# Buffers of the exponentials as slices of one lasting tile, with the order between two exponentials of a slice declared

## The chip, the cores and the metric

The kernel runs on one core of a Trainium2 chip. A core has five engines that run at the same time and wait for each other by semaphores: TensorE (PE, matmuls, with the loading of its weights shown apart as PEld), VectorE (DVE), ScalarE (ACT), GpSimd (POOL) and SyncE (SP, which here issues the DMAs). The metric is device time of one execution in microseconds (us); shorter is better. All times below are of one core.

## The reference

The input x has 2048 rows of 512. The kernel computes `x + s * g`, where s is an attention over the normalized rows and g comes from an MLP over the same rows.

```
xn = layernorm(x)
q  = (xn @ wq) as 32 heads of 16;  k = xn @ wk;  v = xn @ wv      # one k and v for all heads
p  = softmax(q k^T / 4)                                            # 32 heads x 2048 x 2048
s  = (p v, heads side by side) @ wo
h  = xn @ w1 + b1                                                  # 2048 x 1792
g  = silu((h * tanh(softplus(h))) @ w2)
out = x + s * g
```

All numbers are float32.

## The kernel before, in words

**Tiling.** Rows are taken in 4 blocks (C = 512 rows). The 32 heads go in 8 groups of four, so there are 4 x 8 = 32 units (block, group), and each unit goes over the 2048 keys in 16 tiles of 128. One unit and one key tile are one *step*: 512 steps. In each step four score tiles of 128 keys by 512 rows are made, one for each head of the group, exponentiated, and two steps later multiplied with the values.

**What a step issues.** The program is written out by hand in the order in which each engine runs it (manual schedule). For most of the kernel a step holds on TensorE:

- four score matmuls `e` (line 881), each on 64 of the array's rows, into PSUM tiles of the pool `ps_e`, which has three banks;
- four matmuls `m` (line 904) on the other half of the rows, for the running maxima of a later unit, into the pool `ps_m` (three banks); VectorE reduces each of them (line 908);
- a share of one other matrix product, `xps` (line 113), in halves of 64 rows: the projection to q, the two products of the MLP, and the product with `wo`. Such a product is a *group* of 12 or 15 matmuls into the one bank of `ps_x`, cut into chunks of at most 8, and each chunk takes two steps, one for each half of the rows;
- the four value products `pv` of two steps before (line 958), on all rows, which read four exponentials.

The function `waves` interleaves the first three kinds, so that the `e`, `m` and `xps` matmuls of the two row halves run side by side; the value products stand behind them.

ACT takes the exponential of each score tile (line 886, out of PSUM into an SBUF buffer `pt`, 128 x 512). Behind the four exponentials of a step it has one or two other jobs: the stages of the MLP's activation (lines 658, 667, 671), the sigmoid of the gate (727, 732, 737), the reciprocal of the softmax sums (982, 986). Where a group of products ends, ACT or DVE empties its bank between exponentials (lines 597, 652, 715, 719), and once per unit ACT empties the bank of the value products (line 967).

**The buffers of the exponentials.** Before the change, each exponential takes a new tile from a pool with 14 buffers (`NPT = 14`, tag `pt`). The framework that places semaphores makes a new tile wait for everything that used its buffer before: the value products that read it, and the older exponential that wrote it.

```
pt = sb.tile([P, C], F32, tag="pt", name=f"pt{s}_{i}", bufs=NPT)
r = act.activation(pt, e, AF.Exp, scale=0.25)
pt_of[16 * v + k, p, a] = pt
```

In the last 20 steps or so, two of the exponentials of every fourth step go to other buffers (`qh`, `ql`). At the start of the kernel the same 14 buffers hold the first 14 row tiles of x (`load_x`), before any exponential is made.

**The start and the end.** Before the steps begin, a lead of some 90 us (planned with the costs of `Task` objects) normalizes x and computes k, v and the first q. Its weights and the kernel's later ones are loaded, split into a high and a low part, and kept in DRAM. The last 22 steps have no `m` matmuls; the last product with `wo` ends the kernel.

Of the kernel before, what the change touches and what calls it, by code (L numbers as in the profile page):

```python
# [14 lines left out]
F32 = mybir.dt.float32  # L15
# [5 lines left out]
P = 128  # L21
S = 2048
D = 512
# [4 lines left out]
C = 512  # L28
# [15 lines left out]
NPT = 14  # L44
# [75 lines left out]
def block_kernel(ctx: ExitStack, tc: tile.TileContext, x, wq, wk, wv, wo, w1, b1, w2, out):  # L120
    nc = tc.nc
    cp = ctx.enter_context(tc.tile_pool(name="const", bufs=1))
    sb = ctx.enter_context(tc.tile_pool(name="work", bufs=2))
# [65 lines left out]
    nbias = cp.tile([P, NKT], F32, name="nbias")  # L189
    b1c = cp.tile([P, NFT], F32, name="b1c")  # L190
    wbs = cp.tile([P, 5, 2, D], F32R, name="wbs")
    ot_all = cp.tile([P, 4, 2, C], F32R, name="ot_all")

    xr = x.rearrange("o (t p) d -> (o t) p d", p=P)
# [11 lines left out]
    xin = {}  # L206

    def load_x(c):
        for tt in range(4):
            tag, n = ("pt", NPT) if 4 * c + tt < NPT else (("y0", "sc")[tt % 2], 1)  # L210
            xin[c, tt] = sb.tile([P, D], F32, tag=tag, name=f"xin{c}_{tt}", bufs=n)
            sp.dma_start(xin[c, tt], xr[4 * c + tt])

    mvs = cp.tile([P, NKT, 2], F32, name="mvs")
# [26 lines left out]
    def x_scale(t):  # L241
        x_ = xin[divmod(t, 4)]
        if t < 4:
            dve.tensor_scalar(x_, x_, rstd[:, t:t + 1], nbias[:, t:t + 1], op0=ALU.mult, op1=ALU.add)  # L244
        else:
            xn_scale(x_, x_, t)
# [72 lines left out]
    def v_out(c):  # L319
        dve.tensor_copy(vaug[:, 4 * c:4 * c + 4, 0:DH], vp_of[c][:, :, 16:32])  # L320

    load_x(0)
    wkv = sb.tile([P, C], F32, tag="xr", name="wkv", bufs=4)
    wkv = wkv[:, 0:2 * NDT * DH].rearrange("p (a t n) -> p a t n", a=2, t=NDT)
# [56 lines left out]
    def arrived(tag):  # L381
        k, n = todo[tag]
        return k < n and items[tag][k].step + 1 <= (step[0] if lead else max(step[0], busy[0] / STEP_US) + 0.3)
# [459 lines left out]
    def take(n):  # L843
        r = [m1s.popleft() for _ in range(min(n, len(m1s)))]
        queue.extend(r)
        return r

    take(AHEAD)
    for c in range(NC):
        for k in range(3):  # L850
            a = take(2)
# [11 lines left out]
    queue.extend(wo_groups(NC - 1))  # L863

    pt_of = {}
    pv_of = {}
    mb_of = {}
    o_of = {}

    def e_one(s, i):  # L870

        v, r = divmod(s, 16)
        if s < NS - LEAD:
            a, k, p = 1 - s % 2, r - r % 2 + i // 2, i % 2
        else:
            a, k, p = i % 2, r, i // 2
        q = qt_of[v]
        o = 64 * a
        ps, tag = (ps_m, "m") if NS - LEAD <= s and i in ((1, 3) if s < NS - 8 else (3,)) else (ps_e, "e")
        e = ps.tile([P, C], F32, tag=tag, name=f"e{s}_{i}")  # L880
        pe.matmul(e, ks[o:o + 64, P * k:P * (k + 1)], q[o:o + 64, p], start=True, stop=True)  # L881
        if i > 1 and s % 4 == 1 and PAIRS[0] < s < PAIRS[1]:
            pt = sb.tile([P, C], F32, tag=("qh", "ql")[i - 2], name=f"pt{s}_{i}", bufs=1)
        else:
            pt = sb.tile([P, C], F32, tag="pt", name=f"pt{s}_{i}", bufs=NPT)
        r = act.activation(pt, e, AF.Exp, scale=0.25)  # L886
        pt_of[16 * v + k, p, a] = pt
        return r

    m_next = [0, 0]  # L890
# [29 lines left out]
    def c_rows(v):  # L920

        mp = sb.tile([P, 2, 3, 8], F32R, tag="mp", name=f"mp{v}", bufs=2)
        mx = f(mp[:, :, 0])
        w = {}

        def reduce():
            dve.reduce_max(out=mx, in_=mb_of[v].rearrange("p b (a z) -> p a z b", a=2), axis=AX.X)

        def parts():
            dve.tensor_reduce(out=mp[:, :, 1], in_=mx.rearrange("p a (z o) -> p a z o", o=1), axis=AX.X,  # L930
                              op=ALU.max, negate=True)
            dve.tensor_reduce(out=f(mp[:, :, 2]), in_=f(mp[:, :, 0:2]).rearrange("p a s z -> p a z s"), axis=AX.X,
                              op=ALU.add, negate=True)

        def turn():
            cr = w["cr"] = sb.tile([P, 32], F32, tag="cr", name=f"cr{v}", bufs=2)
            dve.transpose(cr, f(mp[:, :, 1:3]).rearrange("p a s z -> p a (s z)"))

        def move():
            q, cr = qt_of[v], w["cr"]  # L940
            for a in range(1, -1, -1):
                r = 64 * a + 48
                for b in range(4):
                    sp_at(0.68)
                    sp.dma_start(f(q[r:r + 2]).rearrange("o p (t b n) -> b o (p t) n", b=4, n=32)[b],
                                 cr[32 * b + 16 * a:32 * b + 16 * a + 16])
        return reduce, parts, turn, move

    def pv(s):
        v, k = divmod(s, 16)  # L950
        if k == 0:
            pv_of[v] = ps_v.tile([P, C], F32, tag="v", name=f"pv{v}")
        o = pv_of[v]
        for p in range(2):
            for a in range(2):
                pt = pt_of.pop((s, p, a))
                j = 2 * p + a
                pe.matmul(o[32 * j:32 * j + 32], vaug[:, k], pt, start=(k == 0), stop=(k == 15))  # L958

# [108 lines left out]
    def task(eng, us, fn, deps=(), **kw):  # L1068
        t = Task(eng, us, fn, deps, **kw)
        plan[eng].append(t)  # L1070
        return t
# [30 lines left out]
    xat = {t: landed(DMA_US) for t in range(4)}  # L1102
    load("wq")
    load_x(1)
    xat.update({t: landed(DMA_US) for t in range(4, 8)})
    load("ws")
    sp.dma_start(b1c, b1.rearrange("(t p) -> p t", p=P))
    load_x(2)
    load_x(3)
    xat.update({t: landed(DMA_US) for t in range(8, 16)})  # L1110
# [18 lines left out]
    for c0, c1 in ((0, 1), (1, 2), (2, 4)):  # L1129
        z = slice(4 * c0, 4 * c1)  # L1130
# [3 lines left out]
        for c in range(c0, c1):  # L1134
            xs, his = [], []
            for t in range(4 * c, 4 * c + 4):
                sc = task(*(("ACT", 0.72), ("DVE", 0.4))[c == 0], lambda t=t: x_scale(t), [nrm])
# [75 lines left out]
    while True:  # L1213
# [21 lines left out]
        s, e, k = min(opts, key=lambda o: o[0])  # L1235
# [5 lines left out]
        if k == "M":  # L1241
# [7 lines left out]
            if vdone[0] == 0 and min(m_next) >= m_need(0):  # L1249
                vdone[0] = 1  # L1250
                r = c_rows(0)
# [20 lines left out]
        elif k == "J":  # L1272
            tag = next((g for g in ("wq", "ws", "wb") if arrived(g) and busy[0] + E0 < s + 0.5), None)
            n = ran[0]
# [16 lines left out]
    while left:  # L1291
        k = next(k for k in left if all(d.end is not None for d in k.deps))
# [6 lines left out]
    for s in range(NS + 2000):  # L1299
        inm = s < NS - LEAD  # L1300
        if inm or cur["chunk"]:
# [4 lines left out]
            def em(k):  # L1306
                n = m_sides(1 - h, k // 2) if inm else 0
                x = deque(lambda i=i: e_one(s, i) for i in range(4))
                y = deque(lambda: m_one(1 - h) for _ in range(n))
                r = [[], []]  # L1310
                for op in EM:
                    if op == "M" and y:
                        r[1 - h].append(y.popleft())
                    elif op == "E":
                        r[1 - h].append(x.popleft())
                r[h] = [lambda: m_one(h) for _ in range(4 - n if inm else 0)]
                return r
# [6 lines left out]
            if s >= 2:  # L1324
                pv(s - 2)
                if (s - 1) % 16 == 0 and s > 1:
                    o_out((s - 17) // 16)
        elif PAIRS[0] <= s < PAIRS[1]:
            due(s)
            if s % 2 == 0:  # L1330
                es = [(s + n // 4, n % 4) for n in range(8)]
                for n in es[:6]:
                    e_one(*n)
                fill(8)
                act_jobs(4)
                for n in es[6:]:
                    e_one(*n)
                for n in range(s - 2, s):
                    pv(n)
                if s % 16 == 0:  # L1340
                    o_out(s // 16 - 1)
            due(s + 0.5)
        else:
# [6 lines left out]
            if s <= NS:  # L1350
                pv(s - 2)
                if s == NS:
                    pv(s - 1)
                if s == NS or (s - 1) % 16 == 0:
                    o_out((s - 16) // 16)
# [4 lines left out]
        if vdone[0] < 8 * NC and min(m_next) >= m_need(vdone[0]):  # L1360
            r = c_rows(vdone[0])
# [20 lines left out]
```

## Time and profile before

| | |
|---|---|
| median of 3 runs | 1609.91 us (1608.72 to 1612.72) |
| the profiled execution | 1610.56 us |
| its span, first to last instruction | 1608.7 us |
| mean granted TensorE clock | 0.998 |
| VectorE, the row maxima of `m` (line 908) | 2048 instructions, 682 ns each in the mean |
| ACT, exponentials (line 886) | 2048 instructions, 606 ns each in the mean |
| TensorE, the products `xps` (line 113) on the chain that ended last | 48% |
| TensorE, the value products (line 958) on it | 31% |

How to read it: the profile has a page of one execution. "Busy" is the time in which an engine runs at least one instruction; instructions of an engine's own sequencer (waits on semaphores, branches, issuing of DMAs) are not busy time and are marked with a q (ACTq, PEldq). Matmul ends are modelled, and matmuls overlap, so that a busy TensorE can still be waiting. The chain that ended last is followed back from the last instruction, at each step to what released it. The order of time lists instructions with start and duration in us; a bracket tells how long the engine was idle before and what ended that. In a view of one line, three numbers with slashes are the shortest, median and longest duration in ns.

### The profile page before, as it was taken

What the parts mean: (1) busy time and instruction counts of PE and PEld (TensorE: products, weight loads), DVE (VectorE), ACT (ScalarE), POOL (GpSimd) and SP (SyncE); (2) the same over time, 40 slices, a digit from 0 to 9 for tenths busy, and PEclk for the clock granted to TensorE, in tenths of its full rate; (3) what the DMA queues carried; (4) which work ended last, traced back from release to release, by engine and by line L of the source; (5) the groups of instructions that cost most, each with busy time, mean ns of one, the idle gap of its engine ahead of it and who ended that gap; (6) DMA issues with size and microseconds to landing.
All of it is one profiled execution on the core that took longest, in us unless ns stands there. A gap on an engine that the chain in (4) does not pass through costs nothing.

```text
span 1608.7 us, 31578 instructions
## 1 busy us (share of the span) xinstructions
PE 1590.6 (99%) x11660; PEld 853.1 (53%) x11660; DVE 1345.7 (84%) x2299; ACT 1292.6 (80%) x2490; POOL 620.0 (39%) x628
## 2 busy tenths in 40 slices
PE   8999999999999999999999999999999999999998
PEld 5455555555555555555555555555555555555543
DVE  8988888888988888888898988888889898888811
ACT  5468788789898778978889787887898878789785
POOL 3786158155365102422524222251251414225312
PEclk9999999999999999999999999999999999999999
DMA  5332133142131315112113231230332213031020
GB/s 161 145 116 83 33 108 119 30 149 76 35 134 61 94 37 173 59 32 87 51 55 96 67 99 37 97 102 16 122 97 83 70 47 106 16 108 45 8 86 27
DMA packets 72778, 127.33 MB, mean 79 GB/s; under 512 B 21488, under 2 KB 34288, under 8 KB 72112
## 3 DMA queue, kind: packets, MB, share of 16 engines
q1 hardware_dynamic: 72624, 125.30, 24.5%
q8 instruction: 93, 1.52, 0.4%
q14 instruction: 61, 0.50, 0.1%
HBM read 76.36 MB, written 27.26 MB: 64 GB/s over the span
## 4 chain that ended last, share of the span: by engine, by line
PE 95%; DVE 2%; ACT 1%; POOL 1%; issue 0%; DMA 0%; SPq 0%; DVEq 0%; ACTq 0%; POOLq 0%
PE xps L113 48%; PE pv L958 31%; PE m L904 8%; PE e L881 5%; PE xps L109 2%; PE kp L293 1%; PE wop L109 1%; DVE mb L908 1%; PE warm L1191 0%; ACT pt L886 0%; ACT xin L198 0%; DMA xin<-in_dram 0%; DVE st L218 0%; POOL hb L157 0%; DVE xin L244 0%
## 5 line engine op out<-in xcount | busy, mean ns | idle before, releaser
L908 DVE TENSOR_REDUCE mb<-m 128x1 f32<-128x512 f32 x2048 | 1272.1, 682 | 189.6 <-PE m L904 162.9
L886 ACT ACTIVATE pt<-e 128x512 f32<-128x512 f32 x2048 | 1068.7, 606 | 255.2 <-PE e L881 243.2
L904 PE MATMUL m<-ks,qt 48*128 48x512 f32 (+1 forms) x2048 | 840.6, 421 | 0.6 <-DVE mb L908 0.2
L881 PE MATMUL e<-qt,ks 64*128 64x512 f32 x2048 | 749.1, 408 | 1.4 <-ACT pt L886 1.4
L958 PE MATMUL pv<-pt,vaug 128*32 128x512 f32 x4096 | 543.8, 604 | 0.0
L904 PEld LDWEIGHTS m<-ks,qt 48*128 48x128 f32 (+1 forms) x2048 | 371.7, 185 | 52.6 <-DVE mb L908 19.0
L881 PEld LDWEIGHTS e<-qt,ks 64*128 64x128 f32 x2048 | 372.9, 186 | 24.3 <-ACT pt L886 17.3
L113 PE MATMUL xps<-xt,ws 64*128 64x512 f32 x1248 | 346.0, 410 | 1.9 <-POOL ws L157 0.9
L113 PE MATMUL xps<-wbs,act 64*128 64x512 f32 x1248 | 337.3, 407 | 0.0
L113 PEld LDWEIGHTS xps<-xt,ws 64*128 64x128 f32 x1248 | 215.1, 185 | 207.5 <-ACT pt L886 135.8
L113 PEld LDWEIGHTS xps<-wbs,act 64*128 64x128 f32 x1248 | 217.6, 185 | 179.9 <-ACT pt L886 112.4
L958 PEld LDWEIGHTS pv<-pt,vaug 128*32 128x32 f32 x4096 | 81.4, 108 | 143.3 <-issue 134.4
L167 POOL TENSOR_SCALAR t<-t 128x512 f32<-128x512 f32 x56 | 34.4, 615 | 316.2 <-ACT t L658 316.1
L157 POOL TENSOR_TENSOR hb<-hb,t 128x512 f32<-128x512 f32 x56 | 72.2, 1289 | 77.8 <-ACT t L671 55.2
L113 PE MATMUL xps<-xt,wq 64*128 64x512 f32 x336 | 93.0, 409 | 0.0
L113 PEld LDWEIGHTS xps<-xt,wq 64*128 64x128 f32 x336 | 57.9, 185 | 55.7 <-ACT pt L886 35.2
L157 POOL TENSOR_TENSOR oc<-oc,sc 128x512 f32<-128x512 f32 (+1 forms) x16 | 20.6, 1288 | 162.4 <-ACT sc L986 96.7
L113 PE MATMUL xps<-wbs,ot_all 64*128 64x512 f32 x288 | 79.3, 407 | 0.0
L113 PEld LDWEIGHTS xps<-wbs,ot_all 64*128 64x128 f32 x288 | 49.4, 184 | 47.1 <-ACT pt L886 29.3
L157 POOL TENSOR_TENSOR hb<-hb,u 128x512 f32<-128x512 f32 x56 | 72.2, 1290 | 4.4
L157 POOL TENSOR_TENSOR act<-hb,act 128x512 fp32r<-128x512 f32 x56 | 72.0, 1286 | 4.7
L157 POOL TENSOR_TENSOR u<-u,t 128x512 f32<-128x512 f32 x56 | 71.8, 1282 | 4.7
(113 smaller groups left out, 807.4 us busy)
## 6 DMA issues: line engine op xcount, KB each, us to landing
ws<-w SPq DMA_DIRECT2D x38, 512.0 KB
wbs<-w SPq DMA_DIRECT2D x36, 512.0 KB
qt<-qh SPq DMA_DIRECT2D x256, 32.0 KB
w<-ws SPq DMA_DIRECT2D x14, 512.0 KB
w<-wbs SPq DMA_DIRECT2D x14, 512.0 KB
wq<-wq SPq DMA_DIRECT2D x13, 512.0 KB
wbs<-wo SPq DMA_DIRECT2D x12, 512.0 KB
rawwb<-in_dram SPq DMA_DIRECT2D x20, 256.0 KB
```

Of the source, the lines that this page charges most:

```text
L109: self.pe.matmul(ps, self.lhs(), self.rhs(), start=(self.k == 0), stop=(self.k == self.tot - 1))
L113: i = self.pe.matmul(ps, self.lhs()[o], self.rhs()[o], start=(self.k == 0 and self.halves == 0), stop=(self.k == self.tot - 1 and self.hal ...
L157: eng.tensor_tensor(out=o, in0=a, in1=b, op=op)
L167: pool.tensor_scalar(o, o, lim, 0.0, op0=ALU.min, op1=ALU.max)
L293: pe.matmul(kp_of[c], wkf[:, dt], xf_of[c][dt // 2][:, dt % 2], start=(dt == 0), stop=(dt == 3))
L881: pe.matmul(e, ks[o:o + 64, P * k:P * (k + 1)], q[o:o + 64, p], start=True, stop=True)
L886: r = act.activation(pt, e, AF.Exp, scale=0.25)
L904: pe.matmul(m, q[o, p, P * t:P * (t + 1)], ks[o, C * kb:C * (kb + 1)], start=True, stop=True)
L908: return dve.reduce_max(out=mb_of[v][:, kb, z:z + 1], in_=m, axis=AX.X)
L958: pe.matmul(o[32 * j:32 * j + 32], vaug[:, k], pt, start=(k == 0), stop=(k == 15))
```

## The change

The 14 pool buffers of the exponentials become slices of one tile `pts` that lasts through the kernel. The program hands the slices out itself: an exponential takes the one that has been free the longest (`pt_free`), and the value product that reads a slice gives it back. For each slice the last exponential is remembered (`pt_last`), and the next exponential in that slice is declared to have no dependency on it, since the value products that read the slice lie between the two. The wait on those value products stays. The first 14 row tiles of x are loaded into the same slices.

```
+    pts = cp.tile([P, NPT, C], F32, name="pts")
...
-            tag, n = ("pt", NPT) if 4 * c + tt < NPT else (("y0", "sc")[tt % 2], 1)
-            xin[c, tt] = sb.tile([P, D], F32, tag=tag, name=f"xin{c}_{tt}", bufs=n)
+            if 4 * c + tt < NPT:
+                xin[c, tt] = pts[:, 4 * c + tt]
+            else:
+                xin[c, tt] = sb.tile([P, D], F32, tag=("y0", "sc")[tt % 2], name=f"xin{c}_{tt}", bufs=1)
...
+    pt_last = {}
+    pt_free = deque(range(NPT))
...
+        z = None
         if i > 1 and s % 4 == 1 and PAIRS[0] < s < PAIRS[1]:
             pt = sb.tile([P, C], F32, tag=("qh", "ql")[i - 2], name=f"pt{s}_{i}", bufs=1)
         else:
-            pt = sb.tile([P, C], F32, tag="pt", name=f"pt{s}_{i}", bufs=NPT)
+            z = pt_free.popleft()
+            pt = pts[:, z]
         r = act.activation(pt, e, AF.Exp, scale=0.25)
-        pt_of[16 * v + k, p, a] = pt
+        if z in pt_last:
+            tc.declare_no_dep(r.ins, pt_last[z].ins, reason="the value products that read the tile lie between")
+        if z is not None:
+            pt_last[z] = r
+        pt_of[16 * v + k, p, a] = pt, z
...
-                pt = pt_of.pop((s, p, a))
+                pt, z = pt_of.pop((s, p, a))
+                if z is not None:
+                    pt_free.append(z)
```

## The prediction

> **What bounds the kernel now.** I read the page first: share of each engine, then the chain that ended last.
>
> ```profile
> PE 1590.6 (99%) x11660; PEld 853.1 (53%) x11660; DVE 1345.7 (84%) x2299; ACT 1292.6 (80%) x2490; POOL 620.0 (39%) x628
> ...
> PE 95%; DVE 2%; ACT 1%; POOL 1%; issue 0%; DMA 0%; SPq 0%; DVEq 0%; ACTq 0%; POOLq 0%
> PE xps L113 48%; PE pv L958 31%; PE m L904 8%; PE e L881 5%; PE xps L109 2%; PE kp L293 1%; PE wop L109 1%; DVE mb L908 1%; PE warm L1191 0%; ACT pt L886 0%; ACT xin L198 0%; DMA xin<-in_dram 0%; DVE st L218 0%; POOL hb L157 0%; DVE xin L244 0%
> ...
> L886 ACT ACTIVATE pt<-e 128x512 f32<-128x512 f32 x2048 | 1068.7, 606 | 255.2 <-PE e L881 243.2
> ```
>
> Read alone, this says that TensorE is full and that the exponentials (ACT, line 886) have 255 us of idle time ahead of them, so that nothing done to them can matter. But a busy PE is not PE at its peak, and matmul ends are modelled, so I went down to the order of time. Next the view of line 886:
>
> ```profile
> L886 ACT ACTIVATE pt<-e x2048: 577/602/695, 92.5 to 1593.5; 128x512 f32<-128x512 f32 x187
> L886 ACTq EVENT_SEMAPHORE  x344: 17/17/38, 108.9 to 1542.9; - x172
> ```
>
> 344 of the 2048 exponentials have an instruction of ACT's sequencer of their own ahead of them. An exponential must wait for its score matmul in any case; I read the 344 as those that have a second wait beside it, nearly all of them on the older exponential in the buffer. Now two steps in a row, in the order of time; the columns are start and duration in us. First one whose exponentials have no such instruction:
>
> ```profile
> 625.01 0.18 PEld L113 LDWEIGHTS xps<-xt,ws 64*128 64x128 f32 x1 [0.84 <-ACT pt L886]
> 625.36 0.40 PE L881 MATMUL e<-qt,ks 64*128 64x512 f32 x1
> 625.80 0.60 ACT L886 ACTIVATE pt<-e 128x512 f32<-128x512 f32 x1 [0.79 <-PE e L881]
> ...
> 626.45 0.18 PEld L881 LDWEIGHTS e<-qt,ks 64*128 64x128 f32 x1
> 626.53 0.41 PE L881 MATMUL e<-qt,ks 64*128 64x512 f32 x1
> 626.87 0.16 PEld L958 LDWEIGHTS pv<-pt,vaug 128*32 128x32 f32 x8 [0.24 <-issue]
> ...
> 627.86 0.18 PEld L113 LDWEIGHTS xps<-xt,ws 64*128 64x128 f32 x1 [0.84 <-ACT pt L886]
> ```
>
> and the next one, which has it ahead of its first exponential (at 628.6):
>
> ```profile
> L886 ACTq EVENT_SEMAPHORE  x1: 17/17/17, 628.6 to 628.6; - x1
> ...
> 628.21 0.40 PE L881 MATMUL e<-qt,ks 64*128 64x512 f32 x1
> 628.70 0.60 ACT L886 ACTIVATE pt<-e 128x512 f32<-128x512 f32 x1 [0.24 <-PE e L881]
> ...
> 629.35 0.18 PEld L881 LDWEIGHTS e<-qt,ks 64*128 64x128 f32 x1
> 629.38 0.46 PE L881 MATMUL e<-qt,ks 64*128 64x512 f32 x1
> 629.77 0.16 PEld L958 LDWEIGHTS pv<-pt,vaug 128*32 128x32 f32 x8 [0.24 <-issue]
> ...
> 630.77 0.18 PEld L113 LDWEIGHTS xps<-xt,ws 64*128 64x128 f32 x1 [0.84 <-ACT hb L652]
> ```
>
> Follow the loop. The first score matmul of the step ends at 625.36 + 0.40 = 625.76; the first exponential starts 0.04 later and ends at 626.40. The step's fourth score matmul needs the PSUM bank that this exponential empties (three banks carry four score tiles): its weight load starts at 626.45, 0.05 after that end. The value products start 0.42 after that load, and the next step's first weight load 0.99 after them. From the first weight load to the next one it is 2.85. In the second step the exponential starts 0.09 after its matmul's end (628.61 to 628.70), everything behind it keeps its distance (fourth load 0.05 after the exponential's end at 629.30, value products 0.42 on, next step 1.00 on), and the step takes 2.91. So in these steps the PE, busy as it looks, stands in a loop with ACT: the delay from the first score matmul's end to the first exponential's start is on the path, one for one.
>
> Not all steps are so. Where the group of products that runs beside has 15 of them (parts of the second MLP product) the PE has more to do per step:
>
> ```profile
> 586.05 0.18 PEld L113 LDWEIGHTS xps<-wbs,act 64*128 64x128 f32 x1 [0.84 <-ACT pt L886]
> ...
> 589.13 0.18 PEld L113 LDWEIGHTS xps<-wbs,act 64*128 64x128 f32 x1 [0.84 <-ACT pt L886]
> ...
> 592.18 0.18 PEld L113 LDWEIGHTS xps<-wbs,act 64*128 64x128 f32 x1 [0.84 <-ACT pt L886]
> ...
> 595.22 0.18 PEld L113 LDWEIGHTS xps<-wbs,act 64*128 64x128 f32 x1 [0.84 <-ACT y L715]
> ...
> L886 ACTq EVENT_SEMAPHORE  x3: 17/17/17, 593.0 to 596.0; - x3
> ```
>
> These are 3.04 to 3.08 apart, the last one with the extra instruction ahead of its first exponential (at 593.0), the others without: there the delay is hidden.
>
> **The change part by part.** *The wait that goes.* Sorting the 485 steps from 99.9 to 1524 us by whether the value products start 0.47 after the first exponential's end (the loop above) gives 359 looped steps and 126 with the PE as their limit. Of the looped ones 167 have the extra instruction ahead of an idle first exponential, the first and the last of them being
>
> ```profile
> 108.45 0.39 PE L881 MATMUL e<-qt,ks 64*128 64x512 f32 x1
> ...
> 108.94 0.60 ACT L886 ACTIVATE pt<-e 128x512 f32<-128x512 f32 x1 [0.27 <-PE e L881]
> ...
> 1478.74 0.40 PE L881 MATMUL e<-qt,ks 64*128 64x512 f32 x1
> ...
> 1479.24 0.60 ACT L886 ACTIVATE pt<-e 128x512 f32<-128x512 f32 x1 [0.23 <-PE e L881]
> ```
>
> and 172 have none, from the first to the last:
>
> ```profile
> 99.92 0.39 PE L881 MATMUL e<-qt,ks 64*128 64x512 f32 x1
> 100.35 0.60 ACT L886 ACTIVATE pt<-e 128x512 f32<-128x512 f32 x1 [0.17 <-PE e L881]
> ...
> 1484.50 0.40 PE L881 MATMUL e<-qt,ks 64*128 64x512 f32 x1
> ...
> 1484.94 0.60 ACT L886 ACTIVATE pt<-e 128x512 f32<-128x512 f32 x1 [0.28 <-PE e L881]
> ```
>
> Over the 167 the delay from matmul end to exponential start is 0.102 us in the mean, over the 172 it is 0.046: 0.056 apart. Their lengths say the same: median 2.907 against 2.852, 0.055 apart. The term is 167 x 0.056 = 9.4 us. Twelve more looped steps have the extra instruction behind an ACT job that ends late; they are worth between nothing and 12 x 0.056 = 0.7, and I take 0.3, as the job hides most of it. The 79 PE-limited steps with the instruction give nothing (above), and so do the instructions ahead of a third exponential, which has ACT work before it.
>
> What is late next? In a step without the instruction the fourth load still starts 0.05 behind the exponential's end, so ACT stays the limit there at 2.85; the 172 such steps show that the PE can run at that length.
>
> One rule of the Trainium skill prices this differently. The row gives the instruction 17 ns; the page "Perfetto Trace Analysis", in the timeline of a sequencer-only instruction, says that the reported window is the execution alone and leaves the wait and the tail out. If the 17 ns were all, the term would be 167 x 0.017 = 2.8 us; the 0.056 measured between the two kinds of step agrees with the page.
>
> *The tile.* The 14 buffers become 14 slices of one lasting tile of the same bytes; the loads of x land in the same slices. No instruction is added: 0. The first exponential in each slice keeps its wait on what the lead did there, 14 of 2048: 0. The free list hands slices out in the order in which the value products gave them back, one step and more before; those products stand in PE's queue ahead of the score matmul that the exponential waits for, so this wait is carried by that one: 0. Dependencies that are kept by tile and not by slice would cost a great deal; that is a rival.
>
> *Waits that others may inherit.* An exponential that waited for an older one told ACT's later instructions that this was done; some may now need a wait of their own. Nearest rows: ACT's other jobs that run between exponentials,
>
> ```profile
> L652 ACT ACTIVATE hb<-xps,b1c 128x512 f32<-128x512 f32 x56 | 38.7, 690 | 9.8 <-PE xps L109 9.8
> ...
> L967 ACT ACTIVATE os<-pv 128x512 f32<-128x512 f32 x31 | 18.7, 603 | 5.1 <-PE pv L958 2.6
> ```
>
> Between 0 and 87 x 0.056 = 4.9 us. I take 0: their buffers come round only after many steps, and jobs of the same chain wait on ACT in between; other jobs run behind the fourth exponential, where ACT then idles 0.23 to 0.28 (rows above) and 0.056 is covered.
>
> Sum: 9.4 + 0.3 = 9.7 off the profiled execution's own 1610.56 us (span 1608.7 and 1.9 around it) gives 1600.9. That execution lies 0.65 above the median 1609.91 of the three; I let the number stand against its own execution.
>
> **The rivals.** (1) *The wait is not what I take it for, or something else takes its place.* If the 344 instructions have another second wait, nothing changes: 1610.6. If 87 evacuations inherit it: 1610.6 - 9.7 + 4.9 = 1605.8, within 0.3%. For: no row names the semaphore of those instructions. Against: 2048 - 344 = 1704 exponentials run without, so score matmul and buffer need no second wait by themselves. 0.10 for both. (2) *ACT is not the bound, so nothing moves*, as the shares at the top say. The Trainium skill, page "Perfetto Trace Analysis", section "Identifying the Most-Contended Engine", has the engine of highest occupancy optimized first, which is not ACT here (PE 99%, DVE 84%, ACT 80%). Against it stand the two steps above, 2.85 and 2.91 with the same PE work. 1610.6, chance 0.02. (3) *Slower: the one lasting tile is tracked whole.* Then the value products, issued behind the step's four exponentials, wait for the last of them instead of starting 0.47 after the first one's end.
>
> ```profile
> 637.30 2.06 ACT L886 ACTIVATE pt<-e 128x512 f32<-128x512 f32 x4 [0.28 <-PE e L881]
> ...
> L437 SPq DMA_DIRECT2D wbs<-w x36: 326/418/1344, 548.1 to 1428.5; - x36
> ```
>
> Four exponentials take 2.06, the first 0.60, so the last ends 1.46 behind the first: products 1.0 later in each of 485 steps, 1610.6 + 485 = some 2096. It decides as soon as a read of one slice waits for a write of another. Against: the ring of wbs is a lasting tile with five slices, refilled by 36 DMAs while products read other slices, and no wait of the PE on those DMAs is listed. 0.04. (4) *All first exponentials gain*, also the PE-limited 79 and the 12: 258 x 0.056 = 14.4, 1596.1. Against: the 3.04 to 3.08 above. 0.05.
>
> **How the numbers follow.** My forecast has 0.79. About 0.3% (4.8 us) is what a measurement of this kernel can tell from no change. Faster: 0.79 + 0.05 = 0.84. Same: 0.10 + 0.02 = 0.12. Slower: 0.04. The range reaches from the fourth rival's 1596.1 to the inherited waits' 1605.8: 1596 to 1606.
>
> **What would show it.** Right: the row of sequencer instructions at line 886's exponential falls from 344 to a handful; the first exponential starts about 0.04 after its matmul in nearly all looped steps, which then take 2.85, and 15-product steps stay at 3.04 to 3.08; ACT's idle time behind score matmuls falls by some 10 us; DVE, POOL and DMA counts stay. Wrong: the row stays; or it falls and steps stay at 2.91, which would put the limit elsewhere; or new sequencer instructions stand at lines 652 and 967; or the value products start behind the fourth exponential.

## The result and the profile after

The changed kernel takes 1599.99 us in the median of six runs (1597.75 to 1602.72), against 1609.84 for six runs of the kernel before: a ratio of 0.9938, 95% interval 0.9925 to 0.9951. The profiled execution takes 1599.22 us, 1597.4 of it in its span.

First the page, with the rows that answer to those shown of before. The engines' shares hardly tell the two kernels apart:

```profile
PE 1579.5 (99%) x11660; PEld 843.1 (53%) x11660; DVE 1345.5 (84%) x2299; ACT 1292.7 (81%) x2490; POOL 620.1 (39%) x628
...
PE 93%; DVE 2%; POOL 2%; ACT 2%; DMA 1%; issue 0%; SPq 0%; DVEq 0%; POOLq 0%; ACTq 0%
...
L893 ACT ACTIVATE pts<-e 128x512 f32<-128x512 f32 x2042 | 1065.5, 605 | 245.7 <-PE e L886 237.2
```

TensorE is "busy" for 11.1 us less, with the same 11660 matmuls: busy time that was waiting. ACT's idle time ahead of the exponentials fell from 255.2 to 245.7. The view of the exponential's line, now 893:

```profile
L893 ACT ACTIVATE pts<-e x2042: 577/600/697, 90.2 to 1582.2; 128x512 f32<-128x512 f32 x186
L893 ACT ACTIVATE pt<-e x6: 579/594/599, 1530.1 to 1553.7; 128x512 f32<-128x512 f32 x6
L893 ACTq EVENT_SEMAPHORE  x3: 17/38/38, 1527.6 to 1530.1; - x3
```

Of the 344 sequencer instructions three are left, all at the end; in the kept trace these three wait for DMAs and stand there in the kernel before as well. And the two steps that the prediction showed, in the order of time (start and duration in us):

```profile
619.40 0.18 PEld L113 LDWEIGHTS xps<-xt,ws 64*128 64x128 f32 x1 [0.84 <-ACT pts L893]
...
619.74 0.40 PE L886 MATMUL e<-qt,ks 64*128 64x512 f32 x1
...
620.18 0.60 ACT L893 ACTIVATE pts<-e 128x512 f32<-128x512 f32 x1 [0.78 <-PE e L886]
...
621.63 0.61 ACT L893 ACTIVATE pts<-e 128x512 f32<-128x512 f32 x1
...
622.25 0.18 PEld L113 LDWEIGHTS xps<-xt,ws 64*128 64x128 f32 x1 [0.84 <-ACT pts L893]
...
622.59 0.40 PE L886 MATMUL e<-qt,ks 64*128 64x512 f32 x1
...
623.03 0.60 ACT L893 ACTIVATE pts<-e 128x512 f32<-128x512 f32 x1 [0.19 <-PE e L886]
...
623.68 0.18 PEld L886 LDWEIGHTS e<-qt,ks 64*128 64x128 f32 x1
...
624.10 0.16 PEld L971 LDWEIGHTS pv<-pts,vaug 128*32 128x32 f32 x8 [0.24 <-issue]
...
625.10 0.18 PEld L113 LDWEIGHTS xps<-xt,ws 64*128 64x128 f32 x1 [0.84 <-ACT hb L655]
```

The second of them was 2.91 long with its first exponential 0.09 behind the matmul's end. Now that exponential starts 0.04 behind it (622.99 to 623.03), the fourth score matmul's weight load still 0.05 behind the exponential's end, the value products 0.42 on, and the step takes 2.85, as the one before it.

Where the 11.3 us between the two spans lie, by the first score matmuls of all steps: the 167 looped steps with the extra instruction gave 9.7, the 12 others 1.1, and the other 306 steps took 0.3 more in sum, 10.5 together. The rest lies outside these steps, and nothing ties it to the change: the lead was 2.3 shorter and the end 1.5 longer, and over the profiles of this study the lead ends anywhere between 96.8 and 102.1 us.

### The profile page after: what moved, and what is told of

Read it like the earlier page. It is cut to its first block, busy times and chain, and to the rows that moved or that the text cites. A ratio compares the mean times of both kernels' runs of the same rounds, so it can differ in the third digit from the quotient of the medians.

```text
span 1597.4 us, 31240 instructions
## 1 busy us (share of the span) xinstructions
PE 1579.5 (99%) x11660; PEld 843.1 (53%) x11660; DVE 1345.5 (84%) x2299; ACT 1292.7 (81%) x2490; POOL 620.1 (39%) x628
## 4 chain that ended last, share of the span: by engine, by line
PE 93%; DVE 2%; POOL 2%; ACT 2%; DMA 1%; issue 0%; SPq 0%; DVEq 0%; POOLq 0%; ACTq 0%
PE xps L113 46%; PE pv L971 31%; PE m L915 8%; PE e L886 5%; PE xps L109 2%; PE wop L109 1%; DVE mb L919 1%; PE warm L1204 1%; PE kp L296 0%; ACT pts L893 0%; DMA w<-wbs 0%; ACT pts L199 0%; POOL hb L157 0%; DVE st L221 0%; DMA pts<-in_dram 0%
## 5 line engine op out<-in xcount | busy, mean ns | idle before, releaser
L893 ACT ACTIVATE pts<-e 128x512 f32<-128x512 f32 x2042 | 1065.5, 605 | 245.7 <-PE e L886 237.2
L886 PE MATMUL e<-qt,ks 64*128 64x512 f32 x2048 | 735.7, 402 | 1.4 <-ACT pt L893 1.4
L971 PE MATMUL pv<-pts,vaug 128*32 128x512 f32 x4084 | 543.8, 604 | 0.0
L886 PEld LDWEIGHTS e<-qt,ks 64*128 64x128 f32 x2048 | 372.9, 186 | 23.0 <-ACT pts L893 12.1
L971 PEld LDWEIGHTS pv<-pts,vaug 128*32 128x32 f32 x4084 | 81.3, 108 | 143.7 <-issue 134.7
```

## The experiments

Each ratio is to executions of the kernel before that were taken with that run (their medians lie between 1609.84 and 1611.81 us). In e5, e6 and e7 some exponentials are left out, so that these three do not compute the result; they only time the steps.

| kernel | median us | ratio to the kernel before, 95% interval |
|---|---|---|
| the change | 1599.99 | 0.9938 [0.9925, 0.9951] |
| e1: slices, no declaration | 1612.55 | 1.001 [1.0, 1.002] |
| e2: the wait at every first exponential | 1616.59 | 1.0035 [1.0024, 1.0047] |
| e3: the wait at every second exponential | 1599.33 | 0.9924 [0.9907, 0.9941] |
| e8: a wait on VectorE at every first exponential | 1600.80 | 0.9932 [0.9908, 0.9955] |
| e10: kernel before, its waits moved to second exponentials | 1601.96 | 0.9944 [0.9927, 0.9961] |
| e7: fourth exponential shorter | 1599.45 | 0.9925 [0.9903, 0.9946] |
| e5: first exponential shorter by an eighth | 1595.03 | 0.99 [0.9876, 0.9924] |
| e6: first exponential shorter by a quarter | 1592.06 | 0.9883 [0.9861, 0.9904] |
| e4: first score matmul one place earlier | 1649.34 | 1.0234 [1.0219, 1.0249] |

**Slices or waits?** The first kernel keeps the lasting tile and drops only the declaration.

```
-        if z in pt_last:
-            tc.declare_no_dep(r.ins, pt_last[z].ins, reason="the value products that read the tile lie between")
```

> The changed kernel without the declaration: the exponentials write slices of the lasting tile, but each may again wait for the older exponential in its slice. In the program 260 first and 81 third exponentials of a step then carry the second wait, as before. Theory (the wait ahead of the first exponential is what cost): 160 of these first ones stand in looped steps with ACT idle before them, so 1600.0 + 160 x 0.056 = 1609, the time of the kernel before. Rival (the tile's place or its bookkeeping gave the gain): 1600.

It has the 344 instructions back (the view of line 893 of this kernel),

```profile
L893 ACTq EVENT_SEMAPHORE  x344: 17/17/38, 111.4 to 1545.8; - x172
```

and the time of the kernel before, 1.001 of it [1.0, 1.002]. The tile's place and the bookkeeping give nothing; the declaration gives everything. It also settles what the rows of before could not name: all but three of the 344 go with the waits on the older exponential. The kept trace names the semaphores and says the same. In the kernel before, 341 of the 344 sequencer instructions wait for the semaphore that TensorE's matmuls raise, and the 341 exponentials behind them for the one that ACT raises itself; the other 1707 exponentials wait for TensorE's alone, as all 2048 do after the change.

**More of the same wait.** The second kernel adds the wait to the changed kernel, at the first exponential of every step.

```
+        if i == 0 and len(exps) > 6:
+            tc.add_manual_dep(r.ins, exps[-6].ins.name, mybir.DependencyInfo(
+                mybir.DependencyClass.Sync, mybir.DependencyReason.DATA), reason="a wait on an older exponential")
+        exps.append(r)
```

> The changed kernel with a wait given to the first exponential of every step, on the exponential made six earlier, done long before. In the program 417 first exponentials carry it as a second wait, 274 of them in looped steps with ACT idle. Theory: 1600.0 + 274 x 0.056 = 1615.3 (to 1617 if the 32 that follow an ACT job cost as well), slower than the kernel before. Rival (the old gain came from elsewhere, such waits are free): 1600.

Two steps of it in the order of time:

```profile
626.15 0.18 PEld L113 LDWEIGHTS xps<-xt,ws 64*128 64x128 f32 x1 [0.84 <-ACT pts L894]
...
626.50 0.40 PE L887 MATMUL e<-qt,ks 64*128 64x512 f32 x1
...
627.00 0.60 ACT L894 ACTIVATE pts<-e 128x512 f32<-128x512 f32 x1 [0.85 <-PE e L887]
...
629.07 0.18 PEld L113 LDWEIGHTS xps<-xt,ws 64*128 64x128 f32 x1 [0.84 <-ACT pts L894]
```

The exponential starts 0.10 behind its matmul, the step takes 2.92, and the kernel 1616.59, where 1615.3 to 1617 was worked out. It is slower than the kernel before, which had the wait at fewer first exponentials. The cost grows with the number of looped steps that carry it.

**The same wait elsewhere.** The third kernel has `i == 1` in place of `i == 0`.

> The same wait given to the second exponential of every step instead; 352 carry it, 251 of them in looped steps. Theory (only the delay between first score matmul and first exponential is on the path; the second score matmul has ended before the second exponential can start): 1600, within 2 us. Rival (each extra sequencer instruction on ACT costs its time, wherever it stands): 1600.0 + 251 x 0.056 = 1614.

```profile
L894 ACTq EVENT_SEMAPHORE  x355: 17/17/38, 99.0 to 1532.6; - x178
...
621.79 0.18 PEld L113 LDWEIGHTS xps<-xt,ws 64*128 64x128 f32 x1 [0.84 <-ACT pts L894]
...
624.64 0.18 PEld L113 LDWEIGHTS xps<-xt,ws 64*128 64x128 f32 x1 [0.84 <-ACT pts L894]
```

More such instructions than the kernel before had, and steps of 2.85: 1599.33. Behind a running exponential the instruction is free here; the number of instructions on ACT's sequencer is not what costs.

**Which of the two waits stands ahead.** The next kernel gives every first exponential a second wait again, but on VectorE (`r = dve.reduce_max(...)`, kept in a list `reds`).

```
+        if i == 0 and len(reds) > 8:
+            tc.add_manual_dep(r.ins, reds[-8].ins.name, mybir.DependencyInfo(
+                mybir.DependencyClass.Sync, mybir.DependencyReason.DATA), reason="a wait on an older maximum")
```

> The changed kernel, where the first exponential of every step gets a second wait on VectorE instead of on ACT: on a maximum eight earlier, done long before. In the program 488 first exponentials then have a sequencer instruction ahead of them, but it carries the wait on VectorE, and the exponential itself waits for its score matmul; with the wait on the older exponential it is the other way round. Theory A (what costs is that the score matmul's wait stands in the sequencer's instruction, so that the exponential starts down its queue only after the matmul has ended): no cost, 1600. Theory B (any second wait ahead of the first exponential costs 0.056): some 320 looped steps with ACT idle, 1618.

```profile
L894 ACTq EVENT_SEMAPHORE  x491: 17/17/38, 94.7 to 1534.9; - x164
...
624.12 0.18 PEld L113 LDWEIGHTS xps<-xt,ws 64*128 64x128 f32 x1 [0.84 <-ACT pts L894]
...
624.47 0.40 PE L887 MATMUL e<-qt,ks 64*128 64x512 f32 x1
...
624.90 0.60 ACT L894 ACTIVATE pts<-e 128x512 f32<-128x512 f32 x1 [0.78 <-PE e L887]
...
626.98 0.18 PEld L113 LDWEIGHTS xps<-xt,ws 64*128 64x128 f32 x1 [0.84 <-ACT pts L894]
```

491 sequencer instructions, the largest number of all, with the exponential 0.03 behind its matmul's end, steps of 2.86, and 1600.80 us: theory A. In the kept trace 488 of them wait for VectorE's semaphore, and every exponential for TensorE's. So a second wait as such costs nothing; with a wait on ACT itself the program puts the wait on the *matmul* into the sequencer's instruction ahead, and the exponential follows only when that instruction is over (628.6 and 628.70 in the prediction's second step). Where the instruction ahead holds the wait that ended long ago, it is over before the matmul is. One thing is left open: from the end of the instruction to the start of the exponential it is 0.045 us in the median in the kernel before, and no run here tells how much of that belongs to the exponential's own wait on ACT's semaphore.

**The kernel before, with waits added.** If place is all, the kernel before should get the whole gain without slices.

```
         r = act.activation(pt, e, AF.Exp, scale=0.25)
+        if i == 1 and len(exps) > 3:
+            tc.add_manual_dep(r.ins, exps[-3].ins.name, mybir.DependencyInfo(
+                mybir.DependencyClass.Sync, mybir.DependencyReason.DATA), reason="a wait on an older exponential")
+        exps.append(r)
```

> The kernel before, its pool of tiles untouched, with a wait added: the second exponential of every step waits for the exponential made three earlier, done long before. ACT then knows that all older ones are done, and no first exponential needs a wait of its own on one: in the program 401 second exponentials carry the second wait, and no first one. Theory (place is all): 1600, the time of the changed kernel, with more extra sequencer instructions than before. Rival (the gain needs the lasting tile, or fewer instructions on ACT's sequencer): 1610, or 1610 and something.

```profile
L887 ACTq EVENT_SEMAPHORE  x404: 17/17/38, 98.5 to 1579.7; - x135
...
619.66 0.18 PEld L113 LDWEIGHTS xps<-xt,ws 64*128 64x128 f32 x1 [0.84 <-ACT pt L887]
...
622.51 0.18 PEld L113 LDWEIGHTS xps<-xt,ws 64*128 64x128 f32 x1 [0.84 <-ACT pt L887]
```

There are 404 such instructions instead of 344, steps of 2.85, and 0.9944 of the time of before [0.9927, 0.9961], which holds the ratio of the change. Waiting more, at a place that is covered, does what the change does.

**Is it the first exponential's bank?** The loop as predicted runs over the end of the first exponential of the step. But the rows name an exponential as what ended the idle time ahead of a step's first weight load, and the fourth one does end at that moment: in the changed kernel at 621.63 + 0.61 = 622.24, with the load at 622.25 (rows of the result). The trace alone does not tell the two apart. So each was made shorter by itself, at the cost of some of its columns; the lines below are those of e5; e6 has 384 in place of 448, and e7 has 384 and `i == 3`. In all three the declaration goes back over every shorter exponential in the slice (in lines that are not shown); 26 second waits in e5 and e6 and 16 in e7 come back even so, all ahead of third exponentials.

```
+        n = 448 if i == 0 and 20 <= s < NS - LEAD - 2 else C
-        r = act.activation(pt, e, AF.Exp, scale=0.25)
+        r = act.activation(pt[:, 0:n], e[:, 0:n], AF.Exp, scale=0.25)
```

> The changed kernel, where the fourth exponential of these steps covers 384 columns (a quarter of that tile left out). Theory (the loop goes over the bank that the first exponential empties, and the fourth only fills time behind it): 1600, within 2 us. Rival, suggested by the rows that name an exponential as what ended the idle time before a step's first weight load: the step's last exponential releases the next step, 1600 - 343 x 0.10 = 1566.

> The changed kernel, where in steps 20 to 487 the first exponential covers 448 of its 512 columns (it leaves an eighth of that tile's exponentials out, and the value products read what the slice held before). By the rows (0.602 us for 512 columns) that takes some 0.05 us off this one exponential; 343 of these steps are looped. Theory, the first exponential's duration is on the path one for one: 1600.0 - 343 x 0.05 = 1583. If another limit stands close behind (the PE's own length of the step; value products stand 0.341 behind the fourth score matmul in looped steps, 0.316 at the least elsewhere): 0.02 a step, 1593. Rival, the loop does not run through this exponential's end: 1600.

> The same with 384 columns, some 0.10 us less. One for one without another limit: 1566. With the PE's limit 0.02 behind: 1593, as with 448 columns. Rival: 1600.

With the fourth exponential a quarter shorter the time is 1599.45 us, nothing gained. With the first one shorter by an eighth it is 1595.03, by a quarter 1592.06. So the path runs over the first and not over the fourth, but it can be shortened by 5 to 8 us only. A step of the kernel with a quarter less, with the first of its maxima (L920), the loads for the fourth `m` (L916) and the fourth `e` (L886), the third and fourth score matmul and the value products:

```profile
625.68 1.29 DVE L920 TENSOR_REDUCE mb<-m 128x1 f32<-128x512 f32 x2 [0.35 <-PE m L916]
...
625.89 1.09 ACT L894 ACTIVATE pts<-e 128x384 f32<-128x384 f32 x2 [0.21 <-PE e L886]
...
626.39 0.40 PE L886 MATMUL e<-qt,ks 64*128 64x512 f32 x1
626.43 0.18 PEld L916 LDWEIGHTS m<-ks,qt 48*128 48x128 f32 x1
626.44 0.18 PEld L886 LDWEIGHTS e<-qt,ks 64*128 64x128 f32 x1
...
626.63 0.39 PE L886 MATMUL e<-qt,ks 64*128 64x512 f32 x1
...
626.95 0.16 PEld L972 LDWEIGHTS pv<-pts,vaug 128*32 128x32 f32 x8 [0.33 <-issue]
...
627.95 0.18 PEld L113 LDWEIGHTS xps<-xt,ws 64*128 64x128 f32 x1 [0.84 <-ACT pts L894]
```

The step (from 625.12) takes 2.83. The fourth score matmul's load still stands 0.05 behind the exponential's end (625.895 + 0.491 = 626.386 for the first of the two in the kept trace, the load at 626.436), but the value products no longer follow it at 0.42: they start 0.51 after it. What stays is their distance from the fourth score matmul, 0.32 (626.63 to 626.95), and that matmul stands 0.24 behind the third, about the pace of the pairs ahead of it (0.23). The medians over the looped steps say the same: in e5 the load comes 1.38 into the step and in e6 1.33 (1.43 in the changed kernel), yet both take 2.83, with the value products 0.32 behind the fourth score matmul in both (0.34 in the changed kernel). That is the limit which the expectations of e5 and e6 named, TensorE's own length of the step, 0.02 behind the loop, with 1593 worked out for both.

A second loop, of the maxima over the three banks of `ps_m`, is a rival for this limit. The load for the fourth `m` stands 0.05 behind the end of the first maximum, which frees its bank (625.684 + 0.692 = 626.376 in the kept trace, the load at 626.428). But it comes 1.32 into the step in the kernel before, in the changed one, in e5 and in e6 alike, 0.19 ahead of its matmul, and that matmul keeps the pace of the pairs (0.23 behind the third score matmul). So these rows show no step in which the maxima hold TensorE up. No kernel here makes a maximum shorter; that TensorE's own length is the next limit is therefore argued from the distances and not shown by an experiment of its own.

**A try at something better.** If the first score matmul stood one pair earlier, ACT could start earlier.

```
-EM = "MEMEMEME"
+EM = "EMEMEMEM"
```

> The changed kernel with the order of a step's matmuls turned, so that the first score matmul stands in the first pair of the step and not in the second. Theory (the loop runs from the step's first weight load over the first score matmul, 0.34 later, to the first exponential): the loop gets shorter by up to a pair's 0.23, until the PE's own length of a looped step is the limit. In the steps without the extra wait the value products stood 0.341 behind the fourth score matmul, against 0.316 at the least elsewhere: 0.02 to 0.03 in 359 steps, 1590 to 1593. Rival (the PE is the limit already, or the maxima's matmuls, now later, become the limit): 1600 or more.

The expectation missed, by 56 us: 1649.34, slower than everything else; the second half of its rival came true. The waits of both kernels, first the changed one, then this (total us, times, longest):

```profile
PEld m L915 <- DVE mb L919: 21.2, 57, 0.8
```

```profile
PEld xps L113 <- DVE mb L919: 289.2, 326, 1.1
...
PEld m L915 <- DVE mb L919: 121.8, 388, 0.8
```

The matmuls `m` come one place later, so the first maximum of a step starts 0.80 into it instead of 0.57 (medians of the looped steps). The load for the fourth `m`, still 0.05 behind that maximum's end, comes at 1.55 instead of 1.32, and its matmul right behind it: now TensorE waits for the bank, and 388 loads of `m` stand behind a maximum where 57 did. The steps that were looped take 2.96 in the mean and the others 3.20, where the changed kernel has 2.86 and 3.09. Here the second loop is at work. No version of this study that computes the result is measurably faster than the change.

## Why the prediction was right

**The bound.** The reading that TensorE's 99% hides a loop with ACT holds. The runs e2 and e1 lengthen it and e5 shortens it through the first exponential alone; e7 shows that the fourth is not on it.

**The size.** The forecast was 1600.9 from an execution of 1610.56; the median is 1599.99. By its terms: 167 x 0.056 = 9.4 was predicted, the same 167 steps gave 9.7, their mean delay falling from 0.102 to 0.043. The 12 others were put at 0.3, at most 0.7, as steps behind an ACT job that ends late, and gave 1.1. That reading was wrong for four of them: there ACT had been idle for 0.56 to 0.77 us, and yet the first exponential started 0.38 to 0.40 behind its matmul, the sequencer instruction being over 0.32 before it (at 207.21, for one). After the change it starts 0.04 to 0.05 behind, and the four gave all of the 1.1; the eight that do stand behind a running job gave nothing. The same four steps have the delay in e1, five others have it in e2, and no looped step has it in e3, e8 and e10. Why the instruction costs so much more in these few is open. The 79 PE-limited steps were put at nothing and gave nothing (0.1 us more in sum). Inherited waits were put at 0: line 655, before 652, has one sequencer instruction as before, and line 980, before 967, has 92 for 90.

```profile
L655 ACT ACTIVATE hb<-xps,b1c x56: 669/691/693, 30.0 to 1473.1; 128x512 f32<-128x512 f32 x56
L655 ACTq EVENT_SEMAPHORE  x1: 17/17/17, 29.9 to 29.9; - x1
...
L980 ACTq EVENT_SEMAPHORE  x92: 17/38/913, 187.1 to 1541.4; - x92
```

That 1600.9 lies within 1 us of the median is in part luck: the steps gave 10.5 and not 9.7, and the lead alone ends up to 5 us earlier or later from one profile to the next.

**What is late next.** The prediction said that the PE can run looped steps at 2.85, and it does. It did not say how close the next limit is: e5 and e6 put it at 2.83, by the distances TensorE's own length.

**The rivals.** That the instructions were another wait falls with e1. That ACT is no bound, as the shares at the top say, falls with the result: the engine with the third highest share gave 0.6% without doing less work (1292.6 and 1292.7 us busy). The Trainium skill's page "Perfetto Trace Analysis", section "Identifying the Most-Contended Engine", has the engine of highest occupancy optimized first, but says for TensorE that the share of busy matmul time is no good measure, which the prediction left out; without TensorE the highest share is VectorE's 84%, and the gain did not come from there either. A tile tracked whole falls, too: the value products start 0.42 behind the fourth score load as before. The fourth rival, a gain in all 258 steps, falls with the PE-limited ones.

**The rule on the sequencer's 17 ns.** The Trainium skill's page "Perfetto Trace Analysis", section "Sequencer-only Instruction (DRAIN, etc)", leaves the wait and the tail of such an instruction out of the reported window. The trace agrees so far as it goes: 17 ns in the row, 0.056 us on the path. The run e8 adds the condition: with the other wait in that instruction no price is measured.

**What was missed of the signs.** ACT's idle time ahead of the exponentials fell by 9.5 us, as the ten that were named; but the part that the views put down to score matmuls, which the sign spoke of, fell only by 6.0, from 243.2 to 237.2. The rest had been put down to other matmuls or to nothing; in the four steps above, for one, the idle time is put down to `m` and `xps`.

## What to carry to other kernels

A busy share of 99% and a chain of waits that names one engine do not exclude that this engine stands in a loop with another: compare two steps of equal work and different length, and follow the distances that stay the same until the one that differs is found. By these runs, a second wait on an instruction costs where the first wait is the one that ends last and has been moved into a sequencer instruction ahead of it; it is free behind running work of the same engine, and free when the instruction ahead carries the wait that is over. Before buffers are rebuilt to get rid of such a wait, try to put it on an instruction that is covered: one added wait did here what the change does.

## What the runs showed of the hardware that was not expected

- A sequencer instruction of 17 ns ahead of an ACT instruction delays it by 0.056 us in the mean (0.102 against 0.046 behind the matmul's end) when it holds the wait on that matmul, by some 0.34 in four steps, and not measurably when it holds a wait that has ended (0.03 behind the matmul's end, 1600.80 us with 491 of them).
- A matmul that waits for a bank need not be shown as idle time: the fourth score matmul of a looped step is recorded with 0.46 us in the step with the extra instruction and 0.41 without, and TensorE's busy time fell by 11.1 us between the two kernels with the same matmuls.
